# Attention and a squared-ReLU layer on one core: the first product taken over pairs of blocks, two tiles turned by DMA, one normalisation a tile, and a new order of transfers

## The chip, the core and the metric

The kernel runs on one core of one Trainium2 chip. The metric is device time in microseconds for one launch, lower is better. The core has a matrix engine (PE, fed by weight loads, PEld), VectorE (DVE), ScalarE (ACT), GpSimd (POOL), which here mostly issues loads and casts them to bf16 on the way, and SyncE (SP), which here issues stores and the transposes that DMA makes. PE accumulates in eight banks of 128 x 512 fp32, and DVE and ACT read those banks.

## The reference

```python
# q, k, v: [4, 8, 768, 64] fp32; w_in: [512, 2048]; w_out: [2048, 512]
scores = q @ k.transpose(0, 1, 3, 2) / sqrt(64)
is_global = pos[None, :] < 8
is_local = (rel >= 0) & (rel < 96)          # rel = query - key
dist = where(is_global & ~is_local, 96, abs(rel))
scores = where(is_global | is_local, scores - slope[h] * dist, -1e9)
a = softmax(scores)
x = (a @ v), heads side by side             # [3072, 512]
out = relu(x @ w_in) ** 2 @ w_out           # [3072, 512] fp32
```

## The kernel before

**Tiles and blocks.** The 3072 tokens are 24 tiles of 128 (numbers 0 to 23, six for each batch), and two tiles make a block of 256 tokens (blocks 0 to 11). A tile's queries see only its own keys, those of the tile before and the eight global ones. Matmuls are in bf16, sums in fp32.

**Attention of a tile.** q, k and v are loaded (L330 for the first six tiles and the weights, L334 from tile 6 on, each load 128 partitions by 512 values; tile 0's q and k come in fp32 from SP, L343). q and k are turned so that the head's 64 numbers lie on partitions: for tiles below `JQK` = 8 by eight matmuls against an identity in two groups (L528, steps `tr`), evicted by DVE or ACT (steps `T.0`, `T.1`), from tile 8 on by one DMA transpose that SP issues (L554, step `T.8`). Then come scores (L618, `sc`; 16 matmuls in four banks for a tile), for the first three tiles preceded by matmuls that add the bias (L597, `bias`), the exponential on ACT (L684, `exp`), a multiply with the mask and ALiBi factors on DVE (L709, `mul`), and the product with v (L767, `pv`). v carries a column of ones, so that each head gives 65 columns, the last being the sum of its probabilities. A half tile is four heads; it has its own bank and its own normalisation on DVE: a reciprocal (L797) and a multiply that also makes bf16 (L798). The result x is turned again: by PE for tiles below `JX` = 8 (L835, `trx`, four matmuls; eviction `xT`), by DMA from tile 8 on (L859).

**The layer.** The first product gives the hidden values of a block transposed: eight steps of 256 hidden units. Block 0, and the first four steps of block 1, take it plainly (L1081, `s1`): 16 matmuls of 256 columns for two steps. The rest takes a two-by-two product in seven smaller products instead of eight (L967, `h`): one pair of halves is that of the 512 inputs, one that of a step's hidden units, and one that of the two tiles of the block. So each of these matmuls has 128 columns (one tile), and a group of four steps has 7 x 8 of them. The products are named p1 to p7; sums of halves of w_in are made once (L907, `isum`), differences of halves of x for each block (L939, `xs`, three instructions). ACT or DVE copies p1 and its like out of a bank (`u`, L453 or L455), a custom DVE instruction adds such a copy to another bank and clips at zero (L1011, `c`), and ACT or DVE squares (L1031, L1033, `q`; for the plain steps relu at L884 or L886 and square at L1117 or L1119). The second product is taken in the same manner for all twelve blocks (`SEVEN`; L1230, `s2.BLOCK.pN.HALF`, 256 columns, 56 matmuls a block), with sums of halves of w_out (L1150, `wsum`) and of the hidden values (L1185, `hsum`, steps `sum`), copies of three products (`part`) and adds (L1305, `o`). A plain form of it stands at L1358 and is not used. Stores of 128 x 512 fp32 go out at L1327 (`st`).

**Order.** Nothing is scheduled by a program at build time: a string `ORDER` lists every step as a word, and `Plan.run` emits the steps in that order. `sc.6.0:567341` is the scores of tile 6 in those banks; `@A` or `@V` puts a step on ACT or DVE; without it, the first engine in the step's list is taken. Each engine executes its own instructions in the order of the string and waits by semaphores for the data and buffers of each. GpSimd and SP issue transfers in order as well, so a transfer whose buffer is not free holds back those behind it. A `gate` word is a small DVE step that marks a v buffer as free for its next load.

GpSimd's loads before the change run in this order: q, k, v of tiles 0 to 5 mixed with the ten transfers of w_in (`win`; steps 0 and 2 in two pieces), then the eight of w_out (`wout`, 256 KB in fp32 each), then v, q, k of tile 6 together (`load.6`), of tile 7, of tile 8 and so on. SP's order is: tile 0's q and k; the turns of tiles 8, 9, 10, 11 (T.8 to T.11) with x of tile 8 between; the first store; then turns and stores mixed.

**The start.** PE runs `NWARM` = 8 matmuls on zeros (L396). DVE makes the identity, the mask `pb` and the slope tiles `sid` (L399 to L414), GpSimd the index table (L391), ACT the factors `E` (L421).

## Time and profile before

| measure | value |
|---|---|
| time of the kernel, three runs | 197.26, 197.51, 197.86 us; median 197.51 |
| span of the profiled execution, first to last instruction | 195.7 us |
| the profiled execution's own time | not given beside its span; the median of the runs is 1.8 us above the span |
| instructions | 6835 |
| granted TensorE clock, mean | 1.000 |
| HBM | 27.26 MB read, 6.29 MB written: 171 GB/s over the span |
| software queue (loads by GpSimd) | 80256 packets, 13.37 MB |
| hardware queue (SP's plain transfers and turns) | 31426 packets, 13.11 MB |

The profile is one execution, taken by the hardware profiler. The span is counted from the first to the last instruction, so what lies around it (the 1.8 us) is not split further here. A share of busy time is an average over the whole span; a stage is read from a window of it. In a row of the groups the numbers behind the bar are busy time of the whole group, mean ns of one instruction, and idle time of the engine just ahead of these. A matmul's own duration there (273 ns for 256 columns) overlaps with its neighbours', since they are pipelined; the pace is read from a run of them in the chain. "POOLq" and "SPq" are the issuing instructions of GpSimd and SP. A row of a transfer gives the length of the issue and, under it, the time from issue to landing.

### The profile page before, as it was taken

To read this page: it belongs to the slowest core of one execution; us is meant where nothing else is said; L and a number is where in the kernel's file an instruction comes from. 1 tells how busy PE (TensorE), PEld (TensorE's weight loads), DVE (VectorE), ACT (ScalarE), POOL (GpSimd) and SP (SyncE) were. 2 spreads that over 40 slices of the span, in tenths; PEclk is the share of its full clock that TensorE was granted. 3 is DMA by queue.
4 is the path that set the end of the run, shared out by engine and by line. 5 is a ranking of instruction groups with operands and counts; after the bars stand their busy time and mean duration, and the time that the engine had idled before them with its cause. 6 is when DMAs were issued, how large, how long until landed. Compare 5 with 4: busy or idle time off the path is not lost.

```text
span 195.7 us, 6835 instructions
## 1 busy us (share of the span) xinstructions
PE 188.5 (96%) x2808; PEld 170.5 (87%) x2808; DVE 179.4 (92%) x437; ACT 161.6 (83%) x338; POOL 75.1 (38%) x93
## 2 busy tenths in 40 slices
PE   7986999999999999999999999999999999999993
PEld 3774999999888989989989989989889999999982
DVE  8569989999999999989999999899999899999982
ACT  6699999999989797999899997587987798986600
POOL 8999784775564502650047080119200000000000
PEclk9999999999999999999999999999999999999999
DMA  7999999999999999999949989999947440152026
GB/s 125 149 150 167 179 193 205 205 162 151 155 150 143 99 177 168 119 100 227 139 79 129 138 74 119 209 168 97 147 113 188 85 136 13 20 193 105 0 91 234
DMA packets 111713, 26.92 MB, mean 138 GB/s; under 512 B 103234, under 2 KB 108866, under 8 KB 111682
## 3 DMA queue, kind: packets, MB, share of 16 engines
q0 software_dynamic: 80256, 13.37, 91.9%
q1 hardware_dynamic: 31426, 13.11, 33.4%
q8 instruction: 22, 0.36, 0.7%
q14 instruction: 9, 0.07, 0.1%
HBM read 27.26 MB, written 6.29 MB: 171 GB/s over the span
## 4 chain that ended last, share of the span: by engine, by line
PE 85%; POOL 6%; DMA 5%; DVE 1%; issue 0%; POOLq 0%; DVEq 0%
PE bank L1230 37%; PE bank L967 32%; PE bank L1081 6%; PE bank L618 5%; PE bank L767 5%; POOL qk_first L330 5%; DMA win<-in_moe_w_in_dram 3%; DMA xT<-x 2%; POOL v L330 2%; PE bank L835 1%; PE bank L528 0%; DVE xs L939 0%; DVE buf L886 0%; DVE hsum L1185 0%; DVE early L1305 0%
## 5 line engine op out<-in xcount | busy, mean ns | idle before, releaser
L684 ACT ACTIVATE buf<-bank 128x512 bf16<-128x512 f32 x76 | 41.5, 613 | 2.8 <-PE bank L618 2.7
L1031 ACT ACTIVATE hs<-buf 128x512 bf16<-128x512 f32 x62 | 37.2, 635 | 2.5 <-DVE buf L1011 2.0
L1230 PEld LDWEIGHTS <-hsum 128*128 128x128 bf16 x384 | 35.3, 98 | 4.0
L453 ACT COPY buf<-bank 128x512 f32<-128x512 f32 (+1 forms) x59 | 32.1, 569 | 7.7 <-PE bank L967 6.1
L1230 PE MATMUL bank<-wsum,hsum 128*128 128x256 bf16 x288 | 38.0, 273 | 0.0
L1011 DVE CUSTOM_DVE_ANT_0 buf<-bank,buf 128x512 f32<-128x512 f32 x49 | 33.0, 682 | 0.8 <-ACT buf L453 0.3
L967 PEld LDWEIGHTS <-qk_first 128*128 128x128 bf16 x504 | 31.1, 98 | 1.4 <-issue 0.3
L967 PEld LDWEIGHTS <-win 128*128 128x128 bf16 x504 | 30.8, 98 | 0.9
L334 POOL DMA_DIRECT2D qk<-in_q_dram x18 | 16.0, 889 | 35.3 <-DMA qkT<-qk 30.0
L1230 PEld LDWEIGHTS <-hs 128*128 128x128 bf16 x288 | 26.3, 98 | 2.7
L1230 PE MATMUL bank<-wout,hs 128*128 128x256 bf16 x192 | 27.3, 273 | 0.0
L334 POOL DMA_DIRECT2D v<-in_v_dram x18 | 16.0, 891 | 23.1 <-PE bank L967 13.1
L967 PE MATMUL bank<-xs,qk_first 128*128 128x128 bf16 x336 | 24.6, 219 | 0.2 <-DVE buf L886 0.2
L967 PE MATMUL bank<-xT,win 128*128 128x128 bf16 x336 | 24.6, 219 | 0.0
L709 DVE TENSOR_TENSOR buf<-buf,E 128x1024 bf16<-128x1024 bf16 x32 | 21.5, 683 | 0.5 <-ACT buf L684 0.5
L798 DVE TENSOR_TENSOR x<-bank,rs 128x256 bf16<-128x256 f32 x48 | 20.4, 425 | 1.7
L767 PE MATMUL bank<-v,buf 128*128 128x65 bf16 x312 | 16.1, 193 | 0.9 <-DMA v<-in_v_dram 0.5
L1185 DVE TENSOR_TENSOR hsum<-hs 128x1024 bf16<-128x1024 bf16 (+1 forms) x26 | 16.4, 642 | 0.3
L334 POOL DMA_DIRECT2D qk<-in_k_dram x18 | 16.1, 897 | 0.6 <-DMA wout<-in_moe_w_out_dram 0.4
L767 PEld LDWEIGHTS <-buf 128*128 128x128 bf16 x312 | 13.9, 98 | 1.8 <-DVE buf L709 0.6
L884 ACT ACTIVATE buf<-bank 128x512 f32<-128x512 f32 x23 | 13.7, 607 | 1.0 <-PE bank L967 1.0
L453 ACT COPY part<-bank 128x256 f32<-128x256 f32 x29 | 11.1, 383 | 3.6 <-PE bank L1230 3.6
(92 smaller groups left out, 349.4 us busy)
## 6 DMA issues: line engine op xcount, KB each, us to landing
out_dram<-buf SPq DMA_DIRECT2D x17, 256.0 KB, 2.7
v<-in_v_dram POOLq DMA_DIRECT2D x24, 128.0 KB, 5.4
qk<-in_q_dram POOLq DMA_DIRECT2D x18, 128.0 KB, 5.0
qk<-in_k_dram POOLq DMA_DIRECT2D x18, 128.0 KB, 5.5
wout<-in_moe_w_out_dram POOLq DMA_DIRECT2D x8, 256.0 KB, 9.7
win<-in_moe_w_in_dram POOLq DMA_DIRECT2D x6, 256.0 KB, 7.1
out_dram<-early SPq DMA_DIRECT2D x5, 256.0 KB, 2.7
qk_first<-in_q_dram POOLq DMA_DIRECT2D x5, 128.0 KB, 4.6
```

What stands on the lines that cost most here:

```text
L334: nc.gpsimd.dma_start(out=dst, in_=src)
L453: nc.scalar.copy(dst, src)
L684: nc.scalar.activation(out=tiles[tag, j, g][:, odd], in_=tiles.pop(("sc", j, odd, g)).rearrange("p a c -> p (a c)"), func=Act.Exp, scale=s ...
L709: nc.vector.tensor_mul(at, tiles.pop(("esc", j, g)), bias)
L767: nc.tensor.matmul(out=po[:, hi, :], lhsT=tiles["at", j, g][:, odd, at * P : (at + 1) * P], rhs=v_sb[kj][:, h, :], start=(i == 0), stop=(i ...
L798: nc.vector.tensor_tensor(out=x[:, 4 * hf : 4 * hf + 4, :], in0=po[:, :, :D], in1=rs.to_broadcast([P, 4, D]), op=Alu.mult,)
L884: nc.scalar.activation(dst, src, Act.Relu)
L967: nc.tensor.matmul(out=tiles["h", blk, g, bank][:, n], lhsT=left_[:, s, k], rhs=right_[:, k], start=opens and n == 0 and k == 0, stop=k == ...
L1011: nc.vector._custom_dve(TENSOR_ADD_SAT, out=hr, in0=src, in1=tiles.pop(("u", blk, g, i)), s0=float("inf"), s1=0.0,)
L1031: nc.scalar.activation(hs, hr, Act.Square)
L1185: nc.vector.tensor_tensor(out=t[:, i, h], in0=t[:, a, h] if isinstance(a, int) else half_a(blk, *a)[:, h], in1=t[:, b, h] if isinstance(b, ...
L1230: nc.tensor.matmul(out=tiles["acc", blk, bank][:, cols], lhsT=left_[:, s], rhs=right_[:, cols], start=first and s == 0, stop=s == NSTEP - ...
```

## The change

All line numbers here are those of the kernel before unless a word says otherwise.

1. **Pairs.** `PAIRS`: blocks 4 and 5, 6 and 7, 8 and 9, 10 and 11 take the first product together. The halves on the token side are now the two blocks instead of the two tiles of one block, so each of these matmuls has 256 columns. A group covers two steps instead of four (`GRP` = 2 there), there are four groups for a pair, and each bank, copy, add and square has 512 columns as before. `xs` takes four instructions for a pair. `NXT` and `NHB` (buffers for turned x and for hidden values) go from 3 to 4.
2. **Plainer early blocks.** `SEVEN1_PART` is empty: block 1's first product is plain throughout. `SEVEN` leaves out block 0, whose second product takes the plain form (32 matmuls of 512 columns, each w_out step used whole, tile by tile).
3. **Tiles 6 and 7 by DMA.** `JQK` and `JX` go from 8 to 6: their q, k and x are turned by SP's transposes.
4. **One normalisation a tile.** `WHOLE`: the two halves of a tile's probability product write two adjacent banks (the eight banks are now one tensor `bank_all`), then one reciprocal of 128 x 8 and one multiply of 128 x 512 follow, behind both halves.
5. **v's load apart.** `load.J.0` is v, `load.J.1` is q and k, and the order string places each. `NV` goes from 10 to 9 buffers of v, `NKT` from 12 to 9 buffers of turned q and k.
6. **The start.** `NWARM` 3 instead of 8; the identity first, the slope tiles `sid` by ACT instead of DVE; the bias matmuls no longer wait for the transposes of their tile, and stand ahead of them.
7. **A new order string**, on every engine.

The constants and the parts that carry the change:

```diff
-    JQK, JX = 8, 8
+    JQK, JX = 6, 6
     JGATE = 9
-    NQ, NKT, NV = 3, 2 * TPB, 10
+    NQ, NKT, NV = 3, 9, 9
...
-    banks = [ps.tile([P, 4 * P], FP32, name=f"bank_{i}", tag=f"bank_{i}") for i in range(NBANK)]
+    bank_all = ps.tile([P, NBANK, 4 * P], FP32, name="bank", tag="bank")
+    banks = [bank_all[:, i] for i in range(NBANK)]
...
-    NHB = 3
-    SEVEN = set(range(NBLK))
+    WHOLE = True
+    PAIRS = ((4, 5), (6, 7), (8, 9), (10, 11))
+    NHB = 4
+    NXT = 4
+    SEVEN = set(range(1, NBLK))
     SEVEN1 = set(range(2, NBLK))
-    SEVEN1_PART = {(1, 1)}
+    SEVEN1_PART = set()
...
-    NWARM = 8
+    NWARM = 3
...
+    nc.vector.tensor_scalar(ident32, pbi[:, 0, :], 0.0, None, op0=Alu.is_equal)
+    for h in range(H):
+        nc.scalar.activation(sid[h], ident32, Act.Copy, scale=float(slopes[h] / scale))
...
-            def emit_load(e, j=j):
+            def emit_load_v(e, j=j):
                 load_v(j)
+
+            def emit_load_qk(e, j=j):
                 load_part(0, j)
                 load_part(1, j)
...
-                    lambda e, gs=gs, f=emit_bias: f(e, gs), deps=[tr],
+                    lambda e, gs=gs, f=emit_bias: f(e, gs), deps=[],
...
+            def emit_whole(e, j=j):
+                tiles["x", j] = lent("x")
+                x, po = tiles["x", j], tiles.pop(("po", j))
+                rs = work.tile([P, 2, 4, 1], FP32, name="rs", tag="rs")
+                nc.vector.reciprocal(rs, po[:, :, :, D : D + 1])
+                nc.vector.tensor_tensor(
+                    out=x.rearrange("p (b a) c -> p b a c", b=2),
+                    in0=po[:, :, :, :D],
+                    in1=rs.to_broadcast([P, 2, 4, D]),
+                    op=Alu.mult,
+                )
...
-    def first_seven(blk, groups=(0, 1)):
+    def first_seven(blk, groups=(0, 1), mate=None):
+        blks = (blk, blk) if mate is None else (blk, mate)
+        wide = mate is not None
+        GRP = 2 if wide else 4
+        W = 2 * P if wide else P
...
         def part_x(kh, sub):
-            return tiles["xT", blk][:, 2 * kh : 2 * kh + 2, sub * P : (sub + 1) * P]
+            t = tiles["xT", blks[sub]][:, 2 * kh : 2 * kh + 2]
+            return t if wide else t[:, :, sub * P : (sub + 1) * P]
...
-        for g in groups:
+        for g in range(4) if wide else groups:
             group(g)
```

The order of transfers after the change, as the words of the string have it:

| queue | order |
|---|---|
| GpSimd | ... k 5, v 4, w_in 1, 2, 6, 0, 2, 0 (the steps 0 and 2 in two pieces), q,k 6, v 5, w_in 5, 7, 4, q,k 7, q,k 8, w_out 6, 0, 1, 2, 3, q,k 9, v 6, w_out 4, 5, 7, q,k 10, v 7, q,k 11, v 8, v 9, q,k 12, v 10, v 11, ... |
| SP | tile 0's q and k, T 6, T 7, T 8, T 9, x 6, T 10, x 7, T 11, x 8, store, x 9, store, ... |

On PE the scores of tile 6 stand behind block 2's first product and ahead of block 0's second; tiles 6 to 11 have their scores and probability products among blocks 0 and 1's second products, earlier in PE's list than before.

## The prediction

> **What bounds the kernel now.** I read the page's engine shares first, then busy time in stretches of ten microseconds, then the chain of waits, then the transfers.

> ```profile
> span 195.7 us, 6835 instructions
> PE 188.5 (96%) x2808; PEld 170.5 (87%) x2808; DVE 179.4 (92%) x437; ACT 161.6 (83%) x338; POOL 75.1 (38%) x93
> ```

> ```profile
> 40.00:50.00 10.00, 10.00 (x118) 9.23 (x116) 9.98 (x21) 9.63 (x21) 6.13 (x7) 1.00 2.30 151
> 100.00:110.00 10.00, 10.00 (x166) 9.08 (x164) 9.67 (x24) 9.47 (x22) 6.14 (x7) 1.00 1.74 99
> ```

> PE is busy in all of each stretch although DVE is nearly full too (columns: PE, weight load, DVE, ACT, POOL, clock, DMA). A busy PE can still be slow, so the chain's pieces give its pace:

> ```profile
> 13.60 6.01 DMA win<-in_moe_w_in_dram
> 19.66 1.07 PE bank L1081 x16
> 35.40 3.13 PE bank L967 x56
> 42.95 2.62 PE bank L1230 x24
> 182.77 9.64 PE bank L1230 x88
> ```

> 3.13/56 is 55.9 ns for a matmul of 128 columns, 2.62/24 is 109.2 for 256, and the 88 at the end run at 109.5, with the clock granted in full. From the landing of the first w_in step (19.6) to the end, PE runs at the pace of its own list. So a shorter list gains what it is shorter by, if nothing makes PE wait; what makes it wait is lost at once.

> **The change part by part: PE's list.** Prices: 55.8 ns for 128 columns, 109.2 for 256; 512 by the same slope (53.4 more per 128 columns) 216.
> - Blocks 4 to 11 in pairs: 7 products x 2 groups x 8 blocks x 8 = 896 matmuls of 128 become 448 of 256: 50.0 to 48.9, -1.1 us.
> - Block 1, second half of the first product, plain: 56 of 128 (3.1) become 32 of 256 (3.5): +0.4.
> - Block 0, second product, plain: 56 of 256 (6.1) become 32 of 512 (6.9): +0.8.
> - Tiles 6 and 7 turned by DMA: 16 + 8 transposes of 128 columns go: -1.3. Their eviction copies go from DVE and ACT.

> Sum -1.26, say -1.3 us.

> **DVE and ACT.**

> ```profile
> L798 DVE TENSOR_TENSOR x<-bank,rs 128x256 bf16<-128x256 f32 x48 | 20.4, 425 | 1.7
> L797 DVE RECIPROCAL rs<-bank 128x4 f32<-128x4 f32 x48 | 8.7, 180 | 0.6
> L1011 DVE CUSTOM_DVE_ANT_0 buf<-bank,buf 128x512 f32<-128x512 f32 x49 | 33.0, 682 | 0.8 <-ACT buf L453 0.3
> ```

> One normalisation a tile: 48 x (0.18 + 0.42) = 29.0 us of DVE become 24 x (0.18 + 0.68) = 20.6, the wide multiply priced like the other 128x512 reads of a bank. The plainer blocks save three custom evictions, four operand sums and seven copies on ACT. PE never waited long for either engine, so I count these at zero, though they make the list safer. The matmul list waits for an eviction chain in the pairs as before.

> **Transfers: the term that decides.** In the kernel before, all weights are issued first, then v, q and k of tiles 6 to 9, and the first turn by DMA is tile 8's, after the last weight has landed. These are answers for single issues (start of the issue, then its time to landing), in order of time:

> ```profile
> L330 POOL DMA_DIRECT2D wout<-in_moe_w_out_dram x1: 696/696/696, 24.2 to 24.2; - x1
> DMA to landing us min/median/max: 8.0/8.0/8.0
> ...
> L330 POOL DMA_DIRECT2D wout<-in_moe_w_out_dram x1: 707/707/707, 31.3 to 31.3; - x1
> DMA to landing us min/median/max: 9.9/9.9/9.9
> ...
> L334 POOL DMA_DIRECT2D v<-in_v_dram x1: 887/887/887, 32.5 to 32.5; - x1
> DMA to landing us min/median/max: 9.5/9.5/9.5
> ...
> L334 POOL DMA_DIRECT2D v<-in_v_dram x1: 873/873/873, 43.4 to 43.4; - x1
> DMA to landing us min/median/max: 6.3/6.3/6.3
> ...
> L554 SPq DMA_TRANSPOSE qkT<-qk x1: 1330/1330/1330, 48.9 to 48.9; - x1
> ```

> The first w_out step lands at 32.2, the eighth at 41.2: 1.28 us each. v of tile 6 lands at 42.0, the ninth load after it at 49.7: 0.85 each. The queue is full there, and the pace is the engines' own:

> ```profile
> DMA packets 6104, 0.79 MB, mean 157 GB/s; under 512 B 6103, under 2 KB 6103, under 8 KB 6103
> ...
> q0 software_dynamic: 6103, 0.77, 241.7%
> ```

> ```profile
> DMA packets 2614, 0.46 MB, mean 153 GB/s; under 512 B 2614, under 2 KB 2614, under 8 KB 2614
> ...
> q0 software_dynamic: 1561, 0.20, 166.4%
> q1 hardware_dynamic: 1053, 0.26, 60.8%
> ```

> The first is 42 to 47 us: 1221 packets a us, loads alone. The second is 54 to 57 us, with tile 9's turn (1053 packets on q1) among loads: 871 a us. A turn therefore costs the loads at least its own packets, 1053/1221 = 0.86 us, and at most the whole shortfall, (3 x 1221 - 1561)/1221 = 1.72. Between them stands what a load loses beside it:

> ```profile
> L334 POOL DMA_DIRECT2D v<-in_v_dram x1: 893/893/893, 48.0 to 48.0; - x1
> DMA to landing us min/median/max: 4.7/4.7/4.7
> ...
> L334 POOL DMA_DIRECT2D v<-in_v_dram x1: 881/881/881, 52.4 to 52.4; - x1
> DMA to landing us min/median/max: 6.1/6.1/6.1
> ```

> 6.1 - 4.7 = 1.4. I take 1.3 for a turn of q and k and half of it (0.4 to 0.9) for a turn of x, which has half the bytes.

> Now the order of GpSimd's queue after the change, from w_in step 4 on: q,k 7; q,k 8; w_out 6, 0, 1, 2, 3; q,k 9; v 6; w_out 4, 5, 7; q,k 10; v 7; q,k 11; v 8. SP turns tiles 6, 7, 8, 9, then x of tile 6, then tile 10, among them. From the same anchor (v of tile 6 at 42.0 in the kernel before):
> - v 6 has three w_out steps fewer ahead of it (-3.8) and eight loads more (+6.8): 45.0, and three turns (3.9): 48.9 (47.6 to 50.2).
> - w_out 7: all weights (41.2), nine loads (+7.65): 48.9, and four turns (5.2): 54.1 (52.3 to 55.7).
> - v 8: 42.0 and fourteen loads (+11.9): 53.9, four turns, one turn of x, half of tile 10's: 60.4 (57.8 to 63.4).

> When does PE want them? The kernel before reaches the probability products of tiles 6 and 8 here:

> ```profile
> 55.04 0.28 PE L767 MATMUL bank<-v,buf 128*128 128x65 bf16 x4
> ...
> 62.56 0.41 PE L767 MATMUL bank<-v,buf 128*128 128x65 bf16 x8
> ```

> Ahead of tile 6's the new list has 72 fewer matmuls of 128, 72 fewer of 256 and ten more of 512 (scores, biases and probability products are equal in number): -4.0 - 7.9 + 2.2 = -9.7, so 45.3. Ahead of tile 8's: 96 and 76 fewer, 32 more: -6.7, so 55.8. The change has moved the attention of tiles 6 to 11 forward and their data back. The second half of block 1's p1, first to read w_out 7, stands 3.9 us behind tile 6's product (four of 256 are 0.4, eight of 65 are 0.25, a group of 16 scores some 0.65, twelve of 512 are 2.6): 49.2.

> So PE waits 3.6 us in all by v 6, 4.9 by w_out 7, 4.6 by v 8. It works in order, so these overlap and the largest counts: 4.9 (at least 52.3 - 49.2 = 3.1, at most 63.4 - 55.8 = 7.6). Behind the first of them stands all of PE's list; DVE holds the sums of w_out 4 to 7 in its order as well, so the multiplies of tiles 7 and 8 queue behind w_out 7 there. SP has x of tile 6 behind tile 9's turn, and tile 10's behind that; POOL's q 9 waits for tile 6's turn, long landed (issued near 28).

> [...]

> **The start.** Bias before the first transposes, three warm-up matmuls for eight, ScalarE making the slope tiles, four loads fewer before the first w_in step (landing near 17 instead of 19.6): a gain or loss of 1 to 2 us at 20 us. It counts for nothing, since PE waits at 54 for landings whose time the start doesn't change; without that cover it would count in full. Splitting v's load costs no DMA (still 24 v loads). The tail is alike: one 256-column eviction and one store.

> **Sum.** 195.7 - 1.3 + 4.9 = 199.3, and 1.8 lies around it (197.51 for the median of the runs less the span): 201.1. Bounds 197.5 - 1.3 + 3.1 = 199.3 and 197.5 - 1.3 + 7.6 = 203.8.

> **Rivals.**
> 1. *The turns slip in for nothing.* Then v 6 lands at 45.0 against 45.3, w_out 7 at 48.9 against 49.2, v 8 at 53.9 against 55.8: all just in time, and the shorter list counts: 197.5 - 1.3 = 196.2, faster. It decides below 0.07 us a turn. For it: the margins come out so close to zero that the order looks made for it. Against: total packets fall with a turn among them. Chance 0.15.
> 2. *A small price.* At 0.4 us a turn the wait is 1.3 and eats the gain: 197.5, no change. Against it, the 0.86 of the packets alone. Chance 0.06.
> 3. *The waits also slow the array.* At the start PE is slow until it has worked a while:

> ```profile
> 1.20 3.59 PE L396 MATMUL bank<-early 128*128 128x512 bf16 x8 [1.20 <-DVE early L385]
> 4.58 1.54 PE L528 MATMUL bank<-ident,plain 128*128 128x128 f32 x8
> ...
> L396 PE MATMUL bank<-early x8: 607/634/634, 1.2 to 4.2; 128*128 128x512 bf16 x8
> ```

> (3.59 - 0.63)/7 is 423 ns for 512 columns, twice 216, for over 3.5 us. If an idle stretch at 45 to 60 us brings that back, half of some 4 us is lost, once: 201.1 + 2 = 203. Against: the waits come in pieces of 1 to 3 us with work between. Chance 0.1. [...]

> **How the numbers follow.** Forecast 201.1 us, chance 0.69 with rival 3 apart (its own range 199.3 to 203.8). I count 0.3% (0.6 us) as no change. Faster 0.15, within 0.06, slower 0.79. For 8 in 10 the range takes in a part of the faster cases: 196.8 to 203.8.

> **What would show it.** In the changed profile: PE gaps between 44 and 62 us before the probability products of tiles 6 to 8 and block 0's plain second product, ended by v or w_out landing; GpSimd's v of tile 6 landing near 49; packets below 1000 a us while both queues work; from 62 on PE dense again, with 256-column first products at 109 ns. I am wrong if PE has no gap there (rival 1), if gaps lie behind evictions instead, or if the early stage alone is late at 40 us.

## The result, and the profile after

| | us | over before, 95% interval |
|---|---|---|
| before, four runs | median 197.47 (197.26 to 197.86) | |
| after, four runs | median 214.79 (213.09, 213.88, 215.7, 219.97) | 1.0827 (1.0767 to 1.0888) |
| span of the profiled execution, before and after | 195.7 and 213.9 | +18.2 us |

The change costs 17.3 us. The ratios, here and in the table of runs below, are taken over the runs that lie within 1.5% of the fastest of the same kernel (219.97 does not), the medians over all runs. First the changed kernel's page: the span, PE's share of it, and the chain that ended last, by engine.

```profile
span 213.9 us, 5776 instructions
PE 193.3 (90%) x2283; PEld 162.9 (76%) x2283; DVE 171.3 (80%) x374; ACT 155.3 (73%) x323; POOL 75.3 (35%) x93
PE 56%; DMA 24%; POOL 8%; DVE 4%; issue 3%; SPq 3%; ACT 2%; DVEq 0%; POOLq 0%; ACTq 0%
```

PE's busy share fell from 96% to 90%, and a quarter of the chain is now waiting for DMA (5% before). What PE waited for (total, times, longest, in us), first the two longest waits of the kernel before that lie behind its start, then those of the changed kernel:

```profile
PE bank L618 <- DVE qkT L455: 0.6, 1, 0.6
PE bank L767 <- DMA v<-in_v_dram: 0.5, 1, 0.5
...
PE bank L615 <- DMA qkT<-qk: 6.1, 2, 3.8
PE bank L1013 <- DVE xs L982: 2.4, 1, 2.4
PE bank L1013 <- DVE early L1058: 2.1, 1, 2.1
```

The row of 6.1 is scores (L615) that wait for turned q and k, twice. Neither v nor w_out is on the changed kernel's list. The answers for the two turns, issued at 36.2 and 50.2 (tiles 7 and 9), and for the loads of v of tile 6 and w_out 7:

```profile
L551 SPq DMA_TRANSPOSE qkT<-qk x1: 1247/1247/1247, 36.2 to 36.2; - x1
...
  PE bank L615: 3.8, 1
DMA to landing us min/median/max: 10.9/10.9/10.9
...
L551 SPq DMA_TRANSPOSE qkT<-qk x1: 1237/1237/1237, 50.2 to 50.2; - x1
...
DMA to landing us min/median/max: 9.1/9.1/9.1
...
L329 POOL DMA_DIRECT2D v<-in_v_dram x1: 903/903/903, 38.6 to 38.6; - x1
...
DMA to landing us min/median/max: 12.3/12.3/12.3
...
L325 POOL DMA_DIRECT2D wout<-in_moe_w_out_dram x1: 696/696/696, 43.5 to 43.5; - x1
...
DMA to landing us min/median/max: 11.9/11.9/11.9
```

Issue start plus the time to landing: tile 7's turn lands near 47.1, tile 9's at 59.3, v 6 at 50.9, w_out 7 at 55.4. Tile 7's scores belong to the same step as tile 6's, so PE stops for the first of these from 43.4 on. Of the 10.9 us of tile 7's turn, four pass before a packet of it moves: the hardware queue has none until 40.2. The record doesn't show what fills them. While the turn of tile 7 is under way the two queues hold (40 to 47 us):

```profile
q0 software_dynamic: 1458, 0.69, 88.1%
q1 hardware_dynamic: 1390, 0.35, 55.8%
```

They moved nearly the same number of packets, although a packet of the loads is 0.69 MB / 1458 = 473 bytes on average here (w_out among them) and one of the turns 252. The turns hold the loads in a second way too: there are buffers for the loaded q and k of three tiles (`NQ`), a turn sets one free when it lands, and GpSimd, which issues in order, waited 51.7 us in all for that (30.0 in the kernel before). One more view is needed for the rest: PE's busy time, matmuls, granted clock, DMA share and GB/s in stretches of 3.41 us, cut where the clock changes:

```profile
39.80:43.21 3.41, 3.41 (x58) 1.00 1.37 149
43.21:46.62 3.41, 0.17 (x8) 1.00 1.50 158
46.62:50.04 3.42, 2.83 (x21) 0.50 1.88 157
50.04:53.45 3.41, 3.41 (x31) 1.00 1.29 204
53.45:56.86 3.41, 3.41 (x32) 1.00 2.27 161
56.86:60.28 3.42, 1.11 (x20) 1.00 1.56 109
60.28:63.69 3.41, 3.41 (x27) 0.50 2.41 156
...
84.17:87.58 3.41, 1.35 (x14) 1.00 1.19 194
87.58:91.00 3.42, 3.42 (x19) 0.50 2.42 154
125.12:128.54 3.42, 2.35 (x39) 1.00 2.41 192
128.54:131.95 3.41, 3.01 (x28) 1.00 1.83 179
142.20:145.61 3.41, 1.40 (x13) 1.00 2.15 191
145.61:149.02 3.41, 3.02 (x20) 0.50 0.88 148
```

Four times a stretch in which PE mostly waited is followed by one with a granted clock of 0.50. Four matmuls of 256 columns took 0.85 us in two of these (at 60.70 and 89.89 of the chain), 213 ns each where 109 is the pace at full clock, so half of the busy time in them is lost: (2.83 + 3.41 + 3.42 + 3.02)/2 = 6.3 us. The span then adds up: the list -1.3, the half clock +6.3, and 18.2 + 1.3 - 6.3 = 13.2 left for waits. By the pages PE's idle time rose from 195.7 - 188.5 = 7.2 to 213.9 - 193.3 = 20.6 us, 13.4 more. The longest gaps behind 25 us are 3.8 at 43, 2.3 at 57, 2.1 at 84, 1.1 and 0.4 at 126 and 131, and 2.4 at 144; the kernel before has none of 0.3 there. (The expectations below count these gaps some 0.2 us longer, from where the next matmul could have begun at the pace of the list.) This is an account of one execution: it says where the time went, not what the time would be if the half clock alone were taken away.

Most of the late gaps have one pattern, in the chain of waits (start, length, what):

```profile
78.30 2.66 SPq L551
81.02 4.27 DMA out_dram<-buf
...
85.75 0.69 DVE early L1058
...
123.11 6.25 DMA out_dram<-early
...
139.16 5.80 DMA xT<-x
...
176.82 3.49 PE bank L1013 x32
```

At 78.3 SP is still issuing turns (L551, tiles 12 and 13); block 0's second store, the third that SP issues, stands behind them and goes out at 81.0, lands at 85.3, and only then is its buffer free for the add of block 2's p5, in front of the custom eviction (L1058, 0.69 us) that PE's next product of block 4 waits for. At 123.1 a store stands behind the x turn of tile 16 in the same way, and the gap of 0.4 at 131 follows. The gap of 1.1 at 126 comes from a store too: ACT waits there for the buffer of one that went out at 120.1 and took 6.3 us to land (the median store of this kind takes 2.3). At 139.2 it is the x turn of tile 19 itself, which the differences of pair 8, 9 need. The last row is the pairs' own pace: 3.49/32 = 109 ns for 256 columns.

### The profile page after: what moved, and what is told of

Its sections match the earlier page's. It is cut to its first block, busy times and chain, and to the rows that moved or that the text cites. A ratio compares the mean times of both kernels' runs of the same rounds, so it can differ in the third digit from the quotient of the medians.

```text
span 213.9 us, 5776 instructions
## 1 busy us (share of the span) xinstructions
PE 193.3 (90%) x2283; PEld 162.9 (76%) x2283; DVE 171.3 (80%) x374; ACT 155.3 (73%) x323; POOL 75.3 (35%) x93
## 3 DMA queue, kind: packets, MB, share of 16 engines
q0 software_dynamic: 80256, 13.37, 83.9%
## 4 chain that ended last, share of the span: by engine, by line
PE 56%; DMA 24%; POOL 8%; DVE 4%; issue 3%; SPq 3%; ACT 2%; DVEq 0%; POOLq 0%; ACTq 0%
PE bank L1273 28%; PE bank L1013 21%; DMA win<-in_moe_w_in_dram 7%; DMA wout<-in_moe_w_out_dram 5%; DMA qkT<-qk 4%; POOL qk_first L325 4%; PE bank L768 3%; DMA out_dram<-early 3%; PE bank L615 3%; DMA xT<-x 3%; SPq L551 2%; POOL v L325 2%; DMA out_dram<-buf 2%; POOL win L325 1%; DVE x L803 1%
## 5 line engine op out<-in xcount | busy, mean ns | idle before, releaser
L329 POOL DMA_DIRECT2D qk<-in_q_dram x18 | 15.9, 886 | 52.2 <-DMA qkT<-qk 51.7
L1013 PEld LDWEIGHTS <-qk_first 128*128 128x128 bf16 x288 | 24.9, 100 | 6.4 <-issue 3.1
L1058 DVE CUSTOM_DVE_ANT_0 buf<-bank,buf 128x512 f32<-128x512 f32 x38 | 25.3, 683 | 3.8 <-ACT early L681 1.7
L1013 PEld LDWEIGHTS <-win 128*128 128x128 bf16 x288 | 24.6, 98 | 4.9 <-issue 2.2
L1013 PE MATMUL bank<-xs,qk_first 128*128 128x256 bf16 (+1 forms) x192 | 23.8, 265 | 2.8 <-DVE xs L982 2.4
L1013 PE MATMUL bank<-xT,win 128*128 128x256 bf16 (+1 forms) x192 | 23.1, 258 | 2.1 <-DVE early L1058 2.1
L615 PE MATMUL bank<-qkT 64*128 64x128 bf16 x192 | 13.2, 224 | 7.7 <-DMA qkT<-qk 6.1
L615 PEld LDWEIGHTS <-qkT 64*128 64x128 bf16 x352 | 10.5, 97 | 12.5 <-DMA qkT<-qk 6.8
L444 ACT COPY part<-bank 128x256 f32<-128x256 f32 x26 | 9.8, 377 | 12.4 <-PE bank L1273 11.8
L803 DVE TENSOR_TENSOR x<-bank,rs 128x512 bf16<-128x512 f32 x24 | 16.6, 692 | 0.9
L681 ACT ACTIVATE early<-bank 128x512 bf16<-128x512 f32 x22 | 12.7, 600 | 6.4 <-DVE buf L1058 3.0
L1348 DVE TENSOR_TENSOR buf<-bank,part 128x256 f32<-128x256 f32 x30 | 12.7, 422 | 5.4 <-PE bank L1273 2.2
```

The source lines that it names most:

```text
L329: nc.gpsimd.dma_start(out=dst, in_=src)
L444: nc.scalar.copy(dst, src)
L615: nc.tensor.matmul(out=tiles["sc", j, odd, g][:, at, :], lhsT=left[j - 1][half, pair, :] if kt else qkT[j % NKT][half, 1, pair, :], rhs=qk ...
L681: nc.scalar.activation(out=tiles[tag, j, g][:, odd], in_=tiles.pop(("sc", j, odd, g)).rearrange("p a c -> p (a c)"), func=Act.Exp, scale=s ...
L803: nc.vector.tensor_tensor(out=x.rearrange("p (b a) c -> p b a c", b=2), in0=po[:, :, :, :D], in1=rs.to_broadcast([P, 2, 4, D]), op=Alu.mult,)
L1013: nc.tensor.matmul(out=tiles["h", blk, g, bank][:, n], lhsT=left_[:, s, k], rhs=right_[:, k], start=opens and n == 0 and k == 0, stop=k == ...
```

## The experiments

Theory A: turns by DMA among the loads are late themselves, make the loads late and hold the stores; PE's waits for them bring the half clock. Rivals: the order of the work or DVE and ACT, not the transfers; and waits that add up without the clock. Each row is against runs of the kernel before on the same chip; "span" and "half" are those of the profiled execution; "half" counts the stretches at half clock that begin after 20 us (turns67_stores has one more, from 17.3 to 20.8).

| run | median us (range) | ratio (95%) | span | half |
|---|---|---|---|---|
| turns67_pe | 213.76 (210.51 to 214.37) | 1.0743 (1.0628 to 1.0858) | 208.7 | 2 |
| stores_first | 214.04 (213.35 to 215.14) | 1.0848 (1.0791 to 1.0904) | 213.4 | 1 |
| turns67_stores | 209.02 (207.83 to 209.81) | 1.0583 (1.0522 to 1.0645) | 207.7 | 0 |
| fill | 219.51 (215.55 to 221.01) | 1.0982 (1.0881 to 1.1083) | 219.2 | 3 |
| half_wout | 210.77 (207.22 to 214.93) | 1.0554 (1.049 to 1.0617) | 207.6 | 1 |
| x1819_pe | 212.26 (211.83 to 213.09) | 1.076 (1.0731 to 1.0789) | 210.1 | 1 |
| quarter_turns | 203.39 (201.37 to 204.34) | 1.0275 (1.0192 to 1.0357) | 202.3 | 0 |
| before_two_turns | 199.62 (199.12 to 200.12) | 1.0109 (1.0083 to 1.0135) | 198.2 | 0 |
| no_pairs | 203.5 (203.02 to 204.21) | 1.0334 (1.0264 to 1.0405) | 201.3 | 0 |
| last_pair | 204.24 (204.15 to 204.8) | 1.0367 (1.0311 to 1.0422) | 202.5 | 0 |
| before_reordered | 206.37 (205.1 to 208.19) | 1.0447 (1.0366 to 1.0529) | 203.8 | 0 |
| all_reordered | 225.1 (224.97 to 225.56) | 1.1423 (1.1362 to 1.1483) | 223.4 | 4 |

**One cause taken away at a time.** Tiles 6 and 7 are turned by PE again:

```diff
-    JQK, JX = 6, 6
+    JQK, JX = 8, 6
...
-T.6 ... T.7
+tr.0.6:6 T.0.6 h.2.1.p7 tr.1.6:2 T.1.6@A ... tr.0.7:6 T.0.7 h.2.1.p4 tr.1.7:2 T.1.7@A
```

> The changed kernel, but q and k of tiles 6 and 7 are turned by PE again (16 transposes of 128 columns, 0.9 us of PE); x of tiles 6 and 7 stays with DMA. Theory A (the loss is in waits for transfers, each followed by a stretch at half clock): the 4.0 us wait for tile 7's turn at 43.2 to 47.2 goes, and the half-clock window behind it. Two turns fewer also bring tile 9's turn (landed at 59.4) some 3.6 us forward, but PE then waits for it from about 52.4, so the gain is what tile 9's turn gains: 3 to 4 us, 210 to 212 us against 214.8. Theory B (the pairs, the wide normalisation or the plain blocks themselves are slow): 0.9 us more, 215.7.

The wait at 43 is gone, the next turn's stays (2.1 at 53), and the late ones too; the time lies between the two expectations:

```profile
PE bank L617 <- DMA qkT<-qk: 2.8, 2, 2.1
PE bank L1015 <- DVE xs L984: 2.8, 2, 2.6
PE bank L1015 <- DVE early L1060: 1.7, 1, 1.7
```

The same for the stores that stand behind turns:

```diff
-T.12 T.13 load.13.0 st.0.0
+st.0.0 T.12 T.13 load.13.0
...
-xT.16:1 ... st.3.0
+st.3.0 xT.16:1
```

> The changed kernel, with two stores taken forward in SP's queue: block 0's second store ahead of the turns of tiles 12 and 13 (it was issued at 81.0, behind them), block 3's first store ahead of x of tile 16 (it was issued at 123.1). Theory A: PE's wait of 2.2 us at 84.2 and the half-clock window behind it (1.7), and the waits of 1.3 and 0.6 at 126 and 131, go: 5 to 6 us, 209 to 210 us. Theory B: no change, 214.8. A third: the stores only change places with the turns, which are then late (scores of tile 12): less than 2 us.

The wait at 84 goes, that at 126 stays (1.2), new ones come at 71.6 (2.1 us), 89.3 (1.5) and 148.1 (1.5), and the time is that of the changed kernel, as the third expectation had it. At 89.3 PE waits for the x turn of tile 11, which now goes out at 83.9 (81.7 in the changed kernel), still behind the turns of tiles 12 and 13. The wait at 71.6 lies ahead of both moved stores, so these did not make it: an x turn issued at 63.9 took 8.8 us, where the changed kernel's, issued at 64.4, took 5.3. Both together:

> The changed kernel with both: tiles 6 and 7's q and k turned by PE, and the two stores forward. Theory A: the gains stand in different waits and add, 3.5 + 5.5: 205 to 207 us. Theory B: 215.7.

Alone they gave 1.0 and 0.8 us, together they bring 214.8 to 209.0, still 2 us above the expectation, with waits left at 54 (tile 9's turn, 1.8), 67, 120, 138 and 143. A wait taken away is worth little while the next transfer is as late. Here are the x turns of tiles 18 and 19, given to PE:

```diff
-        if j < JX:
+        if j < JX or j in (18, 19):
...
-xT.18:0 ... xT.19
+trx.18:3 ... xT.18@A:0 ... trx.19:4 ... xT.19@V
```

> The changed kernel, but x of tiles 18 and 19 is turned by PE (eight transposes of 128 columns, 0.45 us, and two evictions) instead of by DMA. The pair of blocks 8 and 9 waited for tile 19's turn (139.2 to 145.0). If that turn is what ends the wait at 143: the 2.6 us go, and where a half-clock window followed, 1.6 more: 2 to 4 us faster, 211 to 213. If the wait is the pair's need of two blocks' x whatever turns it: no gain, 215.

The wait at 144 goes, those at 43 (3.6), 57 (1.6) and 84 (2.8) stay, and the time is the expected one, 2.5 us less.

**What a turn costs.** The kernel before gets two turns that nobody reads, of w_in steps that lie in SBUF, while w_out is being loaded:

```diff
+        if name in (("win", 7, 0), ("win", 5, 0)):
+            nc.sync.dma_start_transpose(
+                out=qkT[10 + (name[1] == 5)].rearrange("p n a c -> p (n a) c"),
+                in_=dst.rearrange("p k c -> p (k c)"),
+            )
```

> The kernel before with two turns more, and nothing else: when w_in steps 7 and 5 have landed (29.6 and 31.0), SP turns each of them (256 KB, as a tile's q and k) into buffers that tiles 10 and 11 fill later. The results do not use them. They stand among the w_out loads (1.28 us each). At the prediction's price of 1.3 us a turn, v of tile 6 lands at 44.6 instead of 42.0. At what the changed kernel's trace shows (a gap of 1.6 to 2.0 us in the landings for each turn), at 45.5 to 46. The turns themselves: the prediction had no price for their own landing; by the 10.9 and 11.8 us of tiles 7 and 8 beside w_out in the changed kernel, 9 to 12 us. PE wants v of tile 6 at 55 here, so the time stays within 0.5 us of 197.3.

The two turns, v of tile 6 behind them, and both queues at 34 to 40 us:

```profile
L330 SPq DMA_TRANSPOSE qkT<-win x2: 1620/3857/6094, 30.0 to 31.7; - x2
...
DMA to landing us min/median/max: 13.1/13.9/14.8
...
L342 POOL DMA_DIRECT2D v<-in_v_dram x1: 887/887/887, 32.9 to 32.9; - x1
...
DMA to landing us min/median/max: 13.6/13.6/13.6
...
q0 software_dynamic: 958, 0.92, 90.8%
q1 hardware_dynamic: 944, 0.24, 30.7%
```

v 6 lands at 46.5, not 42.0: (46.5 - 42.0)/2 = 2.25 us for each turn. The two turns take 13.1 and 14.8 us, the second behind the first. From 34 to 40 us the two queues moved nearly the same number of packets (958 and 944), and a packet of w_out is 0.92 MB / 958 = 960 bytes against the turn's 254, so the turns got a fifth of the bytes. The time rose by 2.2 us where I had expected nothing: PE stood at w_out for 0.9 at 43.8 and at k for 0.8 at 47.3. The kernel before has less than 4.5 us to spare in its loads there.

Half of w_out left away (steps 0 to 3 stand in for 4 to 7, whose loads are not issued; so this kernel leaves out a part of the layer and is for the time alone):

```diff
-    w_out_sb = [w_out_all[:, s] for s in range(NSTEP)]
+    w_out_sb = [w_out_all[:, s % 4] for s in range(NSTEP)]
```

> The changed kernel without the loads of w_out steps 4 to 7: the second product and the sums of w_out use steps 0 to 3 in their place. 1 MB of the loads before 56 us is gone (5.1 us of the loads' time), order and everything else stay. If turns are late because they share the transfer engines with loads that are queued: tile 9's turn starts 1 us earlier and takes 6 to 7 us instead of 9.1, so it lands near 55 instead of 59.4, and the wait of 2.5 us at 56.7 goes, with the half-clock window that may follow it; the wait at 43 gets shorter by about a us: 4 to 6 us in all, 209 to 211. If turns are slow by themselves: the waits at 43 and 57 stay, 213 to 215.

Tile 9's turn, issued at 50.0, now takes 6.5 us instead of 9.1: it lands at 56.5 and not at 59.3, and the wait at 57 is gone. Tile 7's turn does not gain. The load of w_out 6 ahead of it and those of 4, 5 and 7 beside it are gone, but it is issued at 37.0, takes 10.2 us and lands at 47.2, and PE, which comes to it later, waits 3.1 us.

**All turns at once.** The same order, the same matmuls and loads, but every turn of q and k from tile 6 on moves a quarter. The scores of all heads of these tiles then use the one chunk of q and the one of k that are turned; the other chunks are left out:

```diff
-                    out=T_.rearrange("p n a c -> p (n a) c"),
-                    in_=qk_ring[slot(j)].rearrange("p n c -> p (n c)"),
+                    out=T_[:, 0, :2],
+                    in_=qk_ring[slot(j)].rearrange("p n c -> p (n c)")[:, 384:640],
```

> The changed kernel, same order and same matmuls, but the turns of q and k from tile 6 on move a quarter of the bytes (one chunk of q and one of k; the other chunks are left out and these two are used for all heads). Theory A (the turns among the loads and the stores behind them make the waits, and the waits make the half clock): the turns of tiles 7 and 9 land in 3 to 6 us, the waits at 43 and 57 go, v 6 and w_out 7 land 3 to 5 us earlier, what stands behind turns 12 and 13 goes out earlier; only the turns of x and their neighbours stay late: 197 to 204 us, at most one half window. Rival B (the order, not the turns: loads of q, k, v too late by themselves, or DVE and ACT): waits at 43 to 60 stay over 1 us, 207 us or more. The prediction's own branch of turns for nothing said 196.2.

The page's first two lines, PE's longest waits behind the warm-up, and the turn of tile 7:

```profile
span 202.3 us, 5774 instructions
PE 187.9 (93%) x2281; PEld 160.1 (79%) x2283; DVE 171.6 (85%) x374; ACT 154.9 (77%) x323; POOL 75.2 (37%) x93
...
PE bank L1020 <- DVE xs L989: 1.0, 1, 1.0
PE bank L1280 <- ACT buf L920: 0.9, 1, 0.9
...
L551 SPq DMA_TRANSPOSE qkT<-qk x1: 1171/1171/1171, 34.9 to 34.9; - x1
...
DMA to landing us min/median/max: 6.1/6.1/6.1
```

Tile 7's turn lands at 41.0, six microseconds sooner, v 6 at 47.0 and w_out 7 at 51.1, four sooner each. The turn itself took 6.1 us for a quarter of the bytes, 10.9 whole in the changed kernel. No wait behind the warm-up is above 1.0 us, the clock is full throughout (1.000), and 11.6 us of the span are gone: PE is idle for 14.4 us instead of 20.6 and busy, with the same matmuls, for 187.9 instead of 193.3. This is theory A's number (197 to 204), though the turns of tiles 7 and 9 land in 6.1 and 6.6 us and not in 3 to 6; the rival's 207 or more, with waits at 43 to 60 over 1 us, falls. But it is not 196.2: 5.9 us remain over the kernel before, in many waits of a microsecond and less, with quarter turns, whole turns of x and the stores' order still there. The kernel before holds 16 of these 18 turns of q and k whole and hardly waits, so it is not the bytes alone that cost: it is the bytes in this order, among these loads and ahead of these stores.

**The clock.** To tell waits from what they do to the clock, dummy matmuls fill four of the gaps:

```diff
+                    if at and j == 6:
+                        fill(12, psum(at))
...
+                if j == 9:
+                    fill(8, psum(3))
...
+                    if (blk, g, name) == (4, 3, "p2"):
+                        fill(16, upper[2, "x"])
+                    if (blk, g, name) == (8, 1, "p6"):
+                        fill(20, upper[5, "x"])
```

> The changed kernel, with matmuls ahead of four waits that write only columns which are overwritten or never read: 12 of 512 columns ahead of tile 7's scores, 8 of 512 ahead of tile 9's, 16 and 20 of 256 ahead of the waits at 84 and 143 (1.7 to 2.6 us of work in each wait). They do nothing else. If the half clock comes from PE sitting idle: no half-clock window in the span, and 1.7 each for the second, third and fourth wait; what the first gives (1.4) is waited for again at tile 9's turn. So 4 to 5 us faster, 210 to 211. If the half clock has another cause: same windows, and no change or up to 2 us slower.

In the first three places the stretch behind is at full clock. This is where the changed kernel had 0.17 us of work and then half clock:

```profile
44.34:47.75 3.41, 2.48 (x26) 1.00 1.71 129
47.75:51.17 3.42, 2.51 (x19) 1.00 1.74 178
```

But the time did not fall. In the profiled execution, the slowest of the four, PE met a wait of 2.4 us at 65 and lost the clock behind it, and the fourth filling, at 144, had itself to wait 3.6 us for its bank, with two stretches at half clock behind it. The two fastest runs have a mean granted clock of 0.992 and 0.991, which is one such stretch, and took 218.03 and 215.55 us. So this run shows a full clock behind three gaps that had work in them; it does not show that the time falls with the number of stretches at half clock. The other runs don't agree on that: half_wout took 207.22, 209.34, 212.19 and 214.93 us at 0.999, 0.992, 0.984 and 0.976, but stores_first was fastest (213.35) at 0.976 and slowest (215.14) at 0.992.

**Parts of the change in another order.** I also gave the parts new order strings, the first two near to that of before: the change without pairs and with tiles 6 and 7 turned by PE (`PAIRS = ()`, `JQK, JX = 8, 8`), the same with the last pair (`PAIRS = ((10, 11),)`), the whole change, and the kernel before itself.

> The change without the pairs and with tiles 6 and 7 turned by PE: one normalisation a tile, block 0's second product and all of block 1's first plain, v loaded apart, three warm-up matmuls, slope tiles by ACT. Its order string follows the kernel before: scores of tile 6 stand at the same place of PE's list (103rd group of matmuls; before 104th, the change 77th), most of w_out is loaded ahead of the v of tiles 6 to 11, and SP's first turn is tile 8's. Its list is 1.2 us longer than before's (the plain blocks). Theory A (the loss is PE waiting for transfers that the early attention of the pairs wants too soon): no wait of 2 us, 198 to 200 us. Theory B (these parts are slow in themselves, or the order of before is the only one that works): over 204.

> As no_pairs, with the last pair of the change (blocks 10 and 11) and an order of the same kind. The list is 0.9 us longer than before's. Theory A: a pair at the end wants nothing early, 198 to 200 us. Theory B, if the pairs are the slow part: a quarter of their loss or more, over 202.

> The kernel before in another order string of the same kind: the first stores and some turns forward, w_in steps and loads of tiles 12 to 23 in another order, no part of the change. The list is the same length. 195.5 to 198.5: what is to be had from order alone is the 0.9 us that PE waits between 25 us and the end.

> All parts of the change, with another order string: w_out mixed with the loads of tiles 6 to 9, x of tiles 6 and 7 and the stores forward; the pairs stay, and with them the early attention of tiles 6 to 11 (scores of tile 6 stay 77th). If an order can mend it: under 200. Theory A as I hold it (pairs want two blocks' x, so the attention of tiles 8 to 11 has to stand ahead of the pair 4 and 5, and its transfers have no room): the waits shrink but stay, 204 to 210.

All four missed what theory A, or for the control the count of its waits, had forecast, and last_pair lies where theory B had it (over 202). But the control forbids reading that as the price of a part: the kernel before in a new order takes 206.4, some 9 us more, with nothing changed but the order, and with no wait for a transfer above 0.8. What that time goes to is not shown. What the four bear out: without the early turns and the early attention there is no wait of 2 us and no half clock, and with them in the last order PE again waits for turns (3.7 us in two pieces, and as much for w_out). The 0.7 us between no_pairs and last_pair (203.5 and 204.24) are not clear of the noise: the intervals of the two ratios overlap.

No version beat the kernel before.

## Why the prediction was right in direction and wrong in size

It said 201.1 us (199.3 to 203.8 for its own case), slower because data moved back while their use moved forward. The time was 214.79. Its steps:

- *The list, -1.3 us: right as far as it can be read.* The pairs run at 109 ns for 256 columns, as priced, and the account of the span closes with it to 0.2 us. In quarter_turns, at full clock, PE is busy for 0.6 us less than before (187.9 and 188.5), with the new start in it.
- *One normalisation at 0.18 + 0.68 us: right.* The wide multiply took 692 ns, its reciprocal 203, and no long wait of PE ends at it.
- *A turn costs the loads 1.3 us (0.86 to 1.72): too small.* It was read beside q, k and v, whose packets (0.77 MB / 6103 = 126 bytes) are shorter than the turn's 247. Beside w_out, in the kernel before, it is 2.25. In the changed kernel v 6 landed at 50.9 for 48.9 and w_out 7 at 55.4 for 54.1: with the prediction's other terms, 5.9/3 = 2.0 and 6.5/4 = 1.6 for a turn. Nor is the price a measure of a turn's own landing beside loads: the 256 KB of tile 7's turn took 10.9 us from issue to landing. (The bounds for v 8 do not follow from their own terms: five turns' worth at 0.86 to 1.72 give 58.2 to 62.5, so the upper bound should have been 202.9 and not 203.8. The measured time is far above both.)
- *Who waits: wrong, and this is the step that failed first.* The sum had terms for v 6, w_out 7 and v 8, and none for the landing of a turn; tile 6's was called long landed, 7's and 9's were not asked for. They held the scores, which stand ahead of the probability products, from 43.4 to 47.2 and from 57.1 to 59.4. Behind these waits v 6 and w_out 7 came early enough: PE is busy in all of 50.0 to 56.9. The waits of 4.9 us forecast for 44 to 62 were 6.1, about the right size by another road, and that is luck; with the half clock behind each of them the two places cost 3.1 more.
- *From 62 on PE dense again: wrong.* Four more gaps, at 84, 126, 131 and 144, lost 2.1 + 1.1 + 0.4 + 2.4 = 6.0 us. The prediction had no term for the stores ahead of the tail and did not follow SP's queue behind tile 10's turn, although SP issues in order. At 84 a store stood behind two turns, and the add that needs its buffer, then PE, were late with it; at 144 it was an x turn.
- *Rival 3, the array slowed by waits, +2 us once, chance 0.1: it came true, four times, 6.3 us of busy time.* The reason against it, pieces of 1 to 3 us with work between, fell. The wait of 2.1 us at 84 left 1.35 us of work in its stretch of 3.41, that of 2.4 at 144 left 1.40, and half clock followed both, at 87.58 and 145.61. The prediction did not weigh where in such a stretch a wait falls.
- *Rival 1, turns for nothing, 196.2: not reached.* Quarter turns give 203.4, so even small ones, or what else the order holds, cost 5.9.

Shown by the runs: in this order the bytes of the q and k turns are 11.4 of the 17.3 us (214.79 to 203.39), through waits and through the clock together; taking away a single wait, or the waits of two stores, brought 0.8 to 2.5. Open: how the 11.4 divide between the waits and the clock, since no run takes away the one and leaves the other; how the remaining 5.9 divide among x turns, stores behind turns and the order on the engines; and what each part would be worth in an order as good as that of before.

## What to carry to other kernels

Price a DMA transpose by what its packets stand beside (0.9 to 1.7 us to the loads beside the short packets of q, k and v, 2.25 beside those of w_out), and give its own landing a place in the list of what PE needs, next to the loads that it delays. Follow an in-order queue to its end: block 0's second store stood behind two turns whose issues took 2.0 and 2.7 us, went out at 81.0, and the add that needs its buffer waited 2.1 us. Read the clock behind a wait of PE: here 3.4 us of half clock came behind waits of 2.1 to 3.8 us four times. Look whether the next wait swallows what that costs, and do not expect much from removing one of several in a row.

## What was not expected of the hardware

```profile
58.15:61.57 3.42, 1.60 (x23) 1.00 1.72 129
61.57:64.98 3.41, 3.24 (x51) 1.00 2.05 148
```

In stores_first 0.10 us from 44.50 was followed by half clock too; in fill 1.07 us from 64.82 was, 2.48 from 44.34 was not. So among the stretches at full clock read here those followed by half clock had 1.40 us of work or less, the others 1.60 or more. Behind a stretch that was itself at half clock the clock was full again in the changed kernel (with 2.83 to 3.42 us of work); in fill two stood in a row behind the wait at 144. One stretch at half clock is not accounted for so: that of turns67_stores from 17.3 to 20.8, where the slices of the page (5.19 us each) from 10.4 to 20.8 have PE busy for 80% and 70% or more. Half clock behind some waits and not behind others would fit a kernel that scatters over 7 us (213.09 to 219.97) where the one before scatters over 0.6; that the scatter comes from it was not tested, and the number of stretches alone does not order the four runs: 215.7, 213.09, 219.97 and 213.88 us had mean clocks of 0.968, 0.992, 0.977 and 0.976.

**The turns read here moved nothing at first.** In the changed kernel, beside loads of weights, their first packets came some four microseconds after the issue: at 32.1 for 28.1, at 40.2 for 36.2, and at 54.1 for 50.2. In the kernel before, with only q, k and v among the loads, it was a little over two, at 51.1 for 48.9. It is not explained.

**Both queues nearly stopped for about a microsecond** near 42 and 57 in the changed kernel: they moved 37 GB/s from 41.95 to 42.85, after 172 in the 0.9 us before, and 14 GB/s from 56.85 to 57.85, after 146 from 56.0 to 56.8. A turn was under way each time, and a fetch of instructions (one packet, 0.02 MB) had begun at 40.7 and 55.9, about a microsecond before. It is not explained.
